# An adaLN block with a state-space convolution on one core: the order of its first fifty microseconds

## The chip, the core and the metric

The kernel runs on one core of a Trainium2 chip. The metric is the device time of one execution in microseconds (us). The core has five engines that run their own instruction streams in order: TensorE (PE in the profile, with its weight loads as PEld), VectorE (DVE), ScalarE (ACT), GpSimd (POOL) and SyncE (SP), which here only issues DMA transfers. They wait for each other by semaphores. Before the change the kernel took 1075.2 us, the median of three runs (1074.22, 1075.2 and 1078.04).

## The reference

The input is u, 2048 positions by 640 channels, a condition vector c of 640 and a modulation weight of 640 by 3840. Cut to what matters:

```python
mod = (_silu(c) @ w_mod).reshape(c.shape[0], 6, 1, -1)
sa, ca, ga, sb, cb, gb = (mod[:, i] for i in range(6))
h = _layernorm(u) * (1 + ca) + sa
# S4 convolution, for each channel d a kernel of 128 complex states, of length 2048
P = exp(dt * A * l);  K = einsum("dn,dnl,dn->dl", C, P, dt * B).real
y = irfft(rfft(pad(h)) * rfft(pad(K))) + h * Dskip
x = u + ga * y
h = _layernorm(x) * (1 + cb) + sb
out = x + gb * ((silu(h @ w1) * (h @ w3)) @ w2)     # F = 1728
```

## The kernel before

The kernel has a prelude, a loop of steps that makes the convolution, and an MLP that takes the second half of the time.

**The steps.** The 640 channels are 40 steps of 16 channels. The exponential of a step is split into a slow and a fast factor, so that the kernel K of 2048 positions comes from two tables of 32 and 64 places. For each step s:

- `exps(s)` makes the exponents of two steps at once. PE multiplies logarithms (`lah`, `lal`, `lmh`, `lml`) with constant ramps (`r2`, `r1`, `sel`) into PSUM tiles `pa` (L396) and `pq` (L408); ACT takes the exponential into tile `A`. `pa` and `pq` use the same two PSUM buffers (tag "A"), so `pq` waits until ACT has read `pa`, and the next `pa` until ACT has read `pq`.
- `phases(s)` makes integer phases on POOL (L419, L420); `absph(s)` and `trig(s)` make cosine and sine on ACT (`cs`, `ph`). Sine and exponential are in different ACT tables, and changing between them is an ACT_TABLE_LOAD.
- `tables(s)` on DVE (L438 to L441) multiplies exponentials with cosine and sine into `E` and `A`; `kgen(s)` (L450) and `k_stage1(s)` (L467) on PE turn these into the kernel's spectrum.

**The modulation.** `w_mod` is multiplied with silu(c) in 8 groups of up to 256 columns before the loop and 5 groups of 384 columns in it. `mod_sums` (L267) is one group: five matmuls, one for each 128 rows of c, each with 32 output partitions, at four column places of the PE array in turn; the fifth goes on the first place again. DVE copies the sums (`part`, L269), two small matmuls turn them into columns (L278) and DVE copies these (`cols`, L279). `mod_early(0..4)` make the shift sa and scale ca; `mod_shift` (L284 to L303) then computes sa / (1 + ca), a row `rrow` by PE (`pr`) and a first transform `shift` by PE (`ps`). `mod_early(5..7)` and `mod_gate` make the gate ga.

**The first transform of the input.** `ln1_load(j)` loads one of 16 tiles of 128 positions (seven buffers). `ln1_norm(p)` makes mean and variance of tiles 2p and 2p+1 on DVE (L345, L346, L349), their scale on POOL (L347, L348), and applies both on ACT in place (`x<-x,rs`). `u_stage1(j)` multiplies the tile with a 32-point transform in eight small matmuls (L374), 32 rows by 64 columns of the array each: `pu[0]` (PSUM tag "Z", one buffer) takes rows 0 to 63, `pu[1]` (tag "A") rows 64 to 127. For even j four further matmuls (L366) bring the constant `rrow` into `pu[0]` first, on the same places that the tile's first four need. ACT copies `pu[0]` of an even tile (L377, in the profile L116 `u<-pu`), DVE adds `shift` to the others (L379, L380). The result goes to a scratch in DRAM (L381, 640 KB a tile), from which the loop reads it channel by channel.

**The order.** A tile framework places instructions on each engine. It may move work of one engine past other work by its own priorities. ACT's activations and copies are kept in the order of the program, and so are the phases of steps 1 to 3 on POOL. A block `with tc.issue_after(ins)` holds instructions behind a given one. SP issues transfers in order, each waiting for the buffer that it writes. The gate's weights (`wg`) are loaded into the room of groups 0 to 2 and so wait until these have been multiplied.

Before the change, the prelude reads:

```python
for i, t in enumerate(("pb", "pk", "pb", "pk", "pb")):
    mod_early(i, wm[i], t)
...
mod_shift()
exps(0); ln1_norm(0); exps(2); ln1_norm(1)
phases(1); phases(2); absph(0); trig(0)
u_stage1(0); u_stage1(1); ln1_norm(2)
absph(1); trig(1)
```

What follows is `mod_early(5..7)`, `mod_gate`, `u_stage1(2)`, `u_stage1(3)`, the second half of the parameters (`rest = polar(d1, G)`, partly on POOL, L211 to L259) and the loop. Lines quoted here and in the prediction are those of the kernel before.

Of the kernel before, what the change touches and what calls it, by code (L numbers as in the profile page):

```python
# [9 lines left out]
F32 = mybir.dt.float32  # L10
# [7 lines left out]
P = 128  # L18
# [74 lines left out]
def tile_kernel(ctx: ExitStack, tc: tile.TileContext, a):  # L93
# [96 lines left out]


# [6 lines left out]
    for t, n in ((misc, "misc"), (iota, "iota"), (ident, "ident")):  # L198
        nc.sync.dma_start(t, a[n])

# [61 lines left out]
    def mod_sums(w, pm):  # L262

        n = w.shape[2]
        for k in range(KD):
            g = slice(k % 4 * NA, k % 4 * NA + NA)
            PE.matmul(pm[g, :n], scb[:, k], w[:, k, :], start=(k < 4), stop=(k > 0), tile_position=(0, g.start))  # L267
        part = pm_.tile([P, WC], F32, name="part", bufs=2)
        V.tensor_copy(part[:, :n], pm[:, :n])  # L269
        return part  # L270
# [60 lines left out]
    hpz = pre.enter_context(tc.tile_pool(name="hpz", bufs=2, side="right"))  # L331
    xt = [None] * NT

    def ln1_load(j):
        xt[j] = hpz.tile([P, D], F32, name="x", bufs=7)
        nc.sync.dma_start(xt[j], a["x"][j * P:(j + 1) * P, :])

# [19 lines left out]
    def u_stage1(j):  # L357


        x = xt[j]  # L360
        u = hpz.tile([P, 4, D // 2], F32, name="u", bufs=2)
        pu = [psS.tile([P, 2, 512], F32, name="pu", tag=t, bufs=n) for t, n in (("Z", 1), ("A", 2))]
        one = j % 2 == 0
        for q in range(2 if one else 0):
            for hh in range(2):
                PE.matmul(pu[0][hh * 64:hh * 64 + 64, q, :320], c1[q * NA:q * NA + 1],  # L366
                          rrow[q * NA:q * NA + 1, hh * 320:hh * 320 + 320],
                          start=True, stop=False, tile_position=(q * NA, hh * 64))
        for h in range(2):
            for q in range(2):  # L370
                r0 = (2 * h + q) * NA
                r = slice(r0, r0 + NA)
                for hh in range(2):
                    PE.matmul(pu[h][hh * 64:hh * 64 + 64, q, :320], s1r[r], x[r, hh * 320:hh * 320 + 320],  # L374
                              start=not (one and h == 0), stop=True, tile_position=(r0, hh * 64))
        if one:
            acopy(u[:, :2, :], pu[0][:, :, :320])  # L377
        else:
            V.tensor_tensor(u[:, :2, :], pu[0][:, :, :320], bc(shift, 1, 2), op=OP.add)  # L379
        V.tensor_tensor(u[:, 2:, :], pu[1][:, :, :320], bc(shift, 1, 2), op=OP.add)  # L380
        nc.sync.dma_start(usw[:, 4 * j:4 * j + 4, :], u)  # L381
# [4 lines left out]
    def exps(s, between=()):  # L386
# [18 lines left out]
        for i, (w, rt) in enumerate(((lah, r1), (lal, r1), (lmh, None), (lml, None))):  # L405
            for h, rr, r in rows:
                rv = bc(sel[r, js], 2, NA) if rt is None else rt[r, js, :]
                PE.matmul(pq[h][:, rr, :256], w[r, ch, :], rv,  # L408
                          start=(i == 0), stop=(i == 3), tile_position=(r.start, 0))
        for h in range(2):  # L410
            act(A[h].rearrange("p (r j) s b -> p r j s b", r=2)[:, :, :, 1, :],
                pq[h][:, :, :256].rearrange("p r (j b) -> p r j b", j=8), AF.Exp)
            AA[s + h] = A[h]

# [209 lines left out]
    for j in range(4):  # L624
        ln1_load(j)
# [5 lines left out]
    for i, t in enumerate(("pb", "pk", "pb", "pk", "pb")):  # L631
        mod_early(i, wm[i], t)
    nc.sync.dma_start(s1, a["s1"])
    nc.sync.dma_start(i2, a["i2"])
    nc.sync.dma_start(dz[0:P:NA], a["D"].rearrange("o (g q) -> (o q) g", q=4))
    wg = [w_load(w_room(1, i, n, 1280), 1280 + 256 * i) for i, n in enumerate((256, 256, 128))]
# [3 lines left out]
    mod_shift()  # L640
    exps(0)
    ln1_norm(0)
    exps(2)
    ln1_norm(1)
    phases(1)
    phases(2)
    absph(0)
    trig(0)
    u_stage1(0)
    u_stage1(1)  # L650
    ln1_norm(2)
    absph(1)
    trig(1)
# [360 lines left out]
```

## Time and profile before

| what | value |
| --- | --- |
| median of three runs | 1075.2 us |
| the profiled execution | 1072.31 us |
| its span, first to last instruction | 1070.2 us |
| mean granted TensorE clock | 0.932 |
| PE busy | 975.6 us, 91% |
| DVE busy | 626.6 us, 59% |
| ACT busy | 514.8 us, 48% |
| POOL busy | 266.5 us, 25% |

The profile is of one execution; its time is 2.9 us below the median of the runs. Busy PE counts pipelined matmuls to their ends, so it is not PE at its peak. In a timeline, each row is one or several like instructions: start, time from first start to last end, engine, line, operation, tiles, count, and in brackets the idle time before it with what ended it. ACT's instructions go through two helpers and stand at L113 (activations) and L116 (copies). A fp32 matmul leaves two records. The granted clock of a stretch is a share of PE's full speed. The chain of work that ended last goes from engine to engine through the prelude and the loop, and from about 470 us on stays on PE, in the MLP.

### The profile page before, as it was taken

The page shows a single profiled execution, that of the slowest core. Times are in us where ns is not written, and L with a number is a line of the kernel's source. Part 1 is how long each engine was busy: PE and PEld are TensorE (multiplying, and loading weights), DVE is VectorE, ACT ScalarE, POOL GpSimd, SP SyncE. Part 2 cuts the span into 40 slices and gives each one's busy share as a digit, 9 for nine tenths or more (in the row PEclk, how much of TensorE's full clock was granted, in tenths as well). Part 3 has the DMA queues.
Part 4 walks back from the last instruction along what each step waited for, and adds up shares of the span by engine and source line. Part 5 has one row for each costly group of instructions (what it writes and reads, how often), then busy time and mean ns, then how long its engine had stood idle before and what let it go on. Part 6 is the DMA issues. An engine that isn't in the chain of part 4 may idle for free.

```text
span 1070.2 us, 20346 instructions
## 1 busy us (share of the span) xinstructions
PE 975.6 (91%) x8324; PEld 721.4 (67%) x8324; DVE 626.6 (59%) x1024; ACT 514.8 (48%) x697; POOL 266.5 (25%) x213
## 2 busy tenths in 40 slices
PE   5898887888888899759999999999999999999997
PEld 2444455656665667437778877778777788788886
DVE  4698786787778877655543464443555543533332
ACT  3659585778777873233233432334432334333231
POOL 1633443453345412131211111211111211111110
PEclk9856699988899899869999999999999999999999
DMA  9373593454354549867543364443353233433311
GB/s 276 135 258 125 187 223 110 119 140 130 98 131 130 126 128 227 260 186 221 137 122 87 97 206 120 119 113 97 97 175 99 85 92 95 141 94 99 97 39 49
DMA packets 107040, 146.29 MB, mean 137 GB/s; under 512 B 20836, under 2 KB 62948, under 8 KB 106948
## 3 DMA queue, kind: packets, MB, share of 16 engines
q1 hardware_dynamic: 104500, 140.09, 45.3%
q0 software_dynamic: 1024, 2.49, 0.9%
q10 hardware_dynamic: 1424, 2.43, 0.8%
q8 instruction: 65, 1.06, 0.4%
q14 instruction: 27, 0.22, 0.1%
HBM read 118.76 MB, written 26.21 MB: 135 GB/s over the span
## 4 chain that ended last, share of the span: by engine, by line
PE 74%; DVE 12%; ACT 8%; DMA 3%; issue 2%; POOL 0%; SPq 0%; ACTq 0%; DVEq 0%; POOLq 0%
PE acc L875 17%; PE pg L861 6%; PE pg L862 6%; PE pg L863 6%; PE pu L863 6%; PE pu L862 6%; PE pu L861 6%; PE p L493 5%; PE pz L528 3%; PE pk L450 3%; DVE E L438 2%; PE pt L467 2%; PE pq L408 2%; PE pa L396 2%; DVE A L440 2%
## 5 line engine op out<-in xcount | busy, mean ns | idle before, releaser
L894 POOL TENSOR_TENSOR w<-w,gbr 128x512 f32<-128x512 f32 x55 | 85.1, 1547 | 402.6 <-DMA w<-in_w_dram 383.4
L419 POOL TENSOR_TENSOR ph<-thi,iota 128x1024 int32<-128x1024 int32 x40 | 83.3, 2082 | 194.5 <-DVE A L441 124.2
L861 PE MATMUL pg<-xh,gh 128*128 128x512 f32 x280 | 113.4, 405 | 0.1
L862 PE MATMUL pg<-xl,gh 128*128 128x512 f32 x280 | 111.1, 397 | 0.9 <-DVE xl L834 0.9
L863 PE MATMUL pg<-xh,gl 128*128 128x512 f32 x280 | 110.7, 395 | 0.0
L846 ACT CAST gh<-wg 128x640 fp32r<-128x640 f32 x55 | 40.0, 728 | 145.3 <-PE pg L862 137.8
L847 DVE TENSOR_TENSOR gl<-wg,gh 128x640 fp32r<-128x640 f32 x55 | 51.2, 930 | 92.4 <-ACT gh L846 90.2
L861 PE MATMUL pu<-xh,uh 128*128 128x512 f32 x260 | 102.8, 396 | 0.0
L863 PE MATMUL pu<-xh,ul 128*128 128x512 f32 x260 | 102.8, 396 | 0.0
L862 PE MATMUL pu<-xl,uh 128*128 128x512 f32 x260 | 102.8, 395 | 0.0
L847 DVE TENSOR_TENSOR wl<-w,wh 128x640 fp32r<-128x640 f32 x55 | 47.8, 868 | 89.5 <-ACT wh L846 89.5
L910 DVE TENSOR_TENSOR hf<-pu,sg 128x512 f32<-128x512 f32 x52 | 36.0, 692 | 108.7 <-PE pu L863 107.6
L846 ACT CAST uh<-wu 128x640 fp32r<-128x640 f32 x51 | 37.1, 727 | 111.3 <-issue 70.5
L875 PE MATMUL acc<-wh,hh 128*128 128x512 f32 x224 | 87.7, 391 | 0.0
L875 PE MATMUL acc<-wl,hh 128*128 128x512 f32 x224 | 87.2, 389 | 0.0
L493 PE MATMUL p<-uk,s 128*64 128x256 f32 x640 | 83.8, 407 | 1.3 <-DMA s<-in_s_dram 1.3
L438 DVE TENSOR_TENSOR E<-A,cs 128x1024 f32<-128x1024 f32 x40 | 62.3, 1558 | 37.7 <-ACT cs L113 32.1
L846 ACT CAST wh<-w 128x640 fp32r<-128x640 f32 x55 | 39.9, 726 | 92.2 <-PE acc L875 92.2
L875 PE MATMUL acc<-wh,hl 128*128 128x512 f32 x208 | 81.1, 390 | 0.0
L450 PE MATMUL pk<-E 128*32 128x64 f32 x1280 | 54.3, 247 | 17.8 <-DVE K L458 17.8
L861 PEld LDWEIGHTS pg<-xh,gh 128*128 128x128 f32 x280 | 52.6, 188 | 19.0 <-issue 5.6
L450 PEld LDWEIGHTS pk<-E 128*32 128x32 f32 x1280 | 38.7, 124 | 39.2 <-issue 30.9
(203 smaller groups left out, 2119.2 us busy)
## 6 DMA issues: line engine op xcount, KB each, us to landing
wg<-in_wg_dram SPq DMA_DIRECT2D x55, 320.0 KB
wu<-in_wu_dram SPq DMA_DIRECT2D x51, 320.0 KB
w<-in_w_dram SPq DMA_DIRECT2D x51, 320.0 KB
us<-u SPq DMA_DIRECT2D x16, 640.0 KB
s<-in_s_dram SPq DMA_DIRECT2D x40, 256.0 KB
i<-in_i_dram SPq DMA_DIRECT2D x40, 256.0 KB
uk<-us SPq DMA_DIRECT2D x32, 256.0 KB
zs<-zt SPq DMA_DIRECT2D x32, 256.0 KB
```

The lines of the kernel that those rows point to most:

```text
L419: keep(G.tensor_tensor(p, bc(thi[:, sl], 2, NPH), bc(iota, 1, SD), op=OP.mult))
L438: V.tensor_tensor(E[:, :, 1:3, :], A[:, :, 1:3, :], mid(c), op=OP.mult)
L450: PE.matmul(pk[dq * 32:dq * 32 + 32, g, :], x[:, g * 4 + dq, 1, :], x[:, g * 4 + dq, 0:3:2, :], start=(st == 0), stop=(st == 1), tile_posi ...
L493: PE.matmul(p2[par * 64:par * 64 + 64, pi, c, :], s2[:, pi * 2 + par, c * 64:c * 64 + 64], uk[:, 0:kn + 1:kn, f, :], start=True, stop=True ...
L846: S.copy(hi, src)
L847: V.tensor_tensor(lo, src, hi.bitcast(F32), op=OP.subtract)
L861: PE.matmul(ps, wh, xh, start=(i == 0), stop=False)
L862: PE.matmul(ps, wh, xl, start=False, stop=False)
L863: PE.matmul(ps, wl, xh, start=False, stop=(i == n - 1))
L875: PE.matmul(acc[k], lhs, rhs, start=(f == 0 and i == 0), stop=(f == NFT - 1 and i == len(terms) - 1))
L894: G.tensor_tensor(w2r[:, :512], w2r[:, :512], gbr, op=OP.mult)
L910: V.tensor_tensor(hf, pu, sg, op=OP.mult)
```

## The change

Six things are changed in the text of the kernel:

1. The first four input tiles are loaded ahead of the modulation weights instead of after them.
2. `exps(0)` comes after the first modulation group, `exps(2)` after `ln1_norm(0)`. Groups 1 and 2 are held behind the last matmul of `exps(0)`, groups 3 and 4 behind that of `exps(2)`.
3. `absph` and `trig` of steps 0 and 1 come before `mod_shift`, which stood ahead of the exponents. (`absph(0)` and `trig(0)` work on one step's phases; their ACT instructions are those of before.)
4. `ln1_norm(1)` and `phases(1)`, `phases(2)` move between them.
5. In `mod_sums`, the fifth matmul is two matmuls of half the columns, on the first and the second place.
6. In `u_stage1`, matmuls of `pu[0]` and `pu[1]` are issued in turn; for even tiles the constant rows alternate with those of `pu[1]`, and the tile's matmuls of `pu[0]` follow.

`exps` returns its last matmul for the holds. No operand or size of another operation is changed.

```diff
+    for j in range(4):
+        ln1_load(j)
     wm = [w_load(w, 256 * i) for i, w in enumerate(
...
     def mod_sums(w, pm):
         n = w.shape[2]
-        for k in range(KD):
-            g = slice(k % 4 * NA, k % 4 * NA + NA)
-            PE.matmul(pm[g, :n], scb[:, k], w[:, k, :], start=(k < 4), stop=(k > 0), tile_position=(0, g.start))
+        for k in range(KD - 1):
+            g = slice(k * NA, k * NA + NA)
+            PE.matmul(pm[g, :n], scb[:, k], w[:, k, :], start=True, stop=(k > 1), tile_position=(0, g.start))
+        for i in range(2):
+            g, c = slice(i * NA, i * NA + NA), slice(i * n // 2, (i + 1) * n // 2)
+            PE.matmul(pm[g, c], scb[:, KD - 1], w[:, KD - 1, c], start=False, stop=True, tile_position=(0, g.start))
...
         one = j % 2 == 0
-        for q in range(2 if one else 0):
-            for hh in range(2):
+        group = [(q, hh) for q in range(2) for hh in range(2)]
+        def part(h, q, hh):
+            r0 = (2 * h + q) * NA
+            r = slice(r0, r0 + NA)
+            PE.matmul(pu[h][hh * 64:hh * 64 + 64, q, :320], s1r[r], x[r, hh * 320:hh * 320 + 320],
+                      start=not (one and h == 0), stop=True, tile_position=(r0, hh * 64))
+        for q, hh in group:
+            if one:
                 PE.matmul(pu[0][hh * 64:hh * 64 + 64, q, :320], c1[q * NA:q * NA + 1],
                           rrow[q * NA:q * NA + 1, hh * 320:hh * 320 + 320],
                           start=True, stop=False, tile_position=(q * NA, hh * 64))
-        for h in range(2):
-            for q in range(2):
-                r0 = (2 * h + q) * NA
-                r = slice(r0, r0 + NA)
-                for hh in range(2):
-                    PE.matmul(pu[h][hh * 64:hh * 64 + 64, q, :320], s1r[r], x[r, hh * 320:hh * 320 + 320],
-                              start=not (one and h == 0), stop=True, tile_position=(r0, hh * 64))
+            else:
+                part(0, q, hh)
+            part(1, q, hh)
+        if one:
+            for q, hh in group:
+                part(0, q, hh)
...
-    for j in range(4):
-        ln1_load(j)
...
-    for i, t in enumerate(("pb", "pk", "pb", "pk", "pb")):
-        mod_early(i, wm[i], t)
     nc.sync.dma_start(s1, a["s1"])
     nc.sync.dma_start(i2, a["i2"])
     nc.sync.dma_start(dz[0:P:NA], a["D"].rearrange("o (g q) -> (o q) g", q=4))
+    mod_early(0, wm[0], "pb")
+    last = exps(0)
+    ln1_norm(0)
+    with tc.issue_after(last.ins):
+        mod_early(1, wm[1], "pk")
+        mod_early(2, wm[2], "pb")
+    last = exps(2)
+    with tc.issue_after(last.ins):
+        mod_early(3, wm[3], "pk")
+        mod_early(4, wm[4], "pb")
     wg = [w_load(w_room(1, i, n, 1280), 1280 + 256 * i) for i, n in enumerate((256, 256, 128))]
     for j in range(4, 7):
         ln1_load(j)
     nc.sync.dma_start(prm[:, :, d1], prma[:, :, d1])
-    mod_shift()
-    exps(0)
-    ln1_norm(0)
-    exps(2)
-    ln1_norm(1)
     phases(1)
-    phases(2)
     absph(0)
     trig(0)
+    ln1_norm(1)
+    absph(1)
+    trig(1)
+    mod_shift()
+    phases(2)
     u_stage1(0)
     u_stage1(1)
     ln1_norm(2)
-    absph(1)
-    trig(1)
     for i, t in enumerate(("pb", "pk", "pb")):
         mod_early(5 + i, wg[i], t)
     mod_gate()
```

## The prediction

> **What bounds the kernel now.** I read the page first, then the granted clock, the ScalarE (ACT) timeline of the first 135 us, the waits and the chain there, and stretches of 10 us. The change touches only what is issued before and early in the loop of steps, so the question is how soon that loop gets going. The page, busy tenths in 40 slices of 26.8 us:
>
> ```profile
> span 1070.2 us, 20346 instructions
> ...
> DVE  4698786787778877655543464443555543533332
> ACT  3659585778777873233233432334432334333231
> PEclk9856699988899899869999999999999999999999
> ```
>
> From the fifteenth slice on, PE alone is busy and the change alters nothing. Before that, several engines take turns, and the first slices are ragged. Next the ACT timeline (start, us, instruction, idle before it and what ended that):
>
> ```profile
> 14.67 1.28 ACT L113 ACT_TABLE_LOAD   x1
> 25.13 1.02 ACT L113 ACTIVATE A<-pa 128x1024 f32<-128x1024 f32 x1 [9.18 <-PE pa L396]
> 28.80 1.02 ACT L113 ACTIVATE A<-pa 128x1024 f32<-128x1024 f32 x1 [2.64 <-PE pa L396]
> ...
> 37.42 1.94 ACT L113 ACTIVATE A<-pa 128x1024 f32<-128x1024 f32 x2 [2.92 <-PE pa L396]
> ...
> 47.08 0.67 ACT L116 COPY u<-pu 128x640 f32<-128x640 f32 x1
> ...
> 59.57 0.69 ACT L116 COPY u<-pu 128x640 f32<-128x640 f32 x1 [7.11 <-PE pu L374]
> ...
> 76.98 1.74 ACT L113 ACTIVATE x<-x,rs 128x640 f32<-128x640 f32 x2 [3.85 <-DVE rs L349]
> ```
>
> ACT stands 9.18, 2.64 and 2.92 us for the `pa` matmuls of the exponents, since PE does five modulation groups between them; 7.11 us for the transform of tile 2; and 3.85 us for the norm of tiles 8 and 9. From 76.98 to 103 it has no wait over 0.4 us. Then PE, in stretches (PE, weight loads, DVE, ACT, POOL busy; clock; DMA share; GB/s):
>
> ```profile
> 10.00:20.00 10.00, 9.08 (x41) 3.80 (x37) 8.39 (x23) 5.12 (x9) 2.98 (x2) 1.00 1.09 339
> 20.00:30.00 10.00, 10.00 (x44) 5.28 (x46) 2.40 (x10) 2.05 (x2) 0.00 (x0) 1.00 0.98 294
> ...
> 40.00:50.00 10.00, 8.89 (x64) 3.83 (x60) 5.12 (x12) 9.84 (x12) 6.50 (x8) 0.67 0.25 91
> 50.00:60.00 10.00, 9.63 (x62) 3.63 (x60) 9.74 (x15) 2.86 (x4) 8.02 (x8) 0.50 0.31 108
> 60.00:70.00 10.00, 9.89 (x119) 4.47 (x120) 8.95 (x14) 8.23 (x12) 1.48 (x3) 0.50 0.90 311
> ```
>
> And two groups of PE's timeline (one modulation group of five matmuls, ten records; eight matmuls of the transform, sixteen records):
>
> ```profile
> 16.56 1.92 PE L267 MATMUL pm<-uk,scb 128*32 128x256 f32 x10 [0.25 <-DVE cols L279]
> 60.04 1.64 PE L374 MATMUL pu<-x,misc 32*64 32x320 f32 x16
> ```
>
> DVE is nearly idle from 20 to 30 (2.40 busy) and half idle from 40 to 50 (5.12), then full from 50 to 100: its work is there too late rather than too large. A modulation group takes 1.92 at 16.56, and two take 3.62 at 43.12 under a granted 0.50 to 0.67, so the 1.00 of the first stretches is no faster; I use one set of PE durations.
>
> **The change, step by step** (times of the profiled execution; after = my walk through the built order).
>
> *x ahead of its weights.* 1.31 MB of x now lies before the modulation weights. They landed at 9.82 (PE's first wait); at 339 and 227 GB/s (stretches 10 to 20 and 0 to 10) they come 3.9 to 5.8 later, 13.7 to 15.6. The group behind takes 1.5, done by 17.1 at worst; the exponents' first matmul needs DVE's `lml`, 16.8. Cost 0 to 0.3; I take 0. On SP the four issues took 3.02 at 12.03; the weights' issues move behind them by that, inside the transfers' delay. The gate weights on SP overwrite weights of groups 0 to 2 and now wait for them until about 25 instead of 18 to 22.6; behind them stand x tiles 4 to 6 and the second parameters. 1.94 MB at 339 GB/s and 2 us of issue make tile 6 land at 32.5; DVE wants it from 35. The 1.57 MB of parameters come near 37; POOL used them at 48.53. Hidden, with 2.5 us to spare; without that cover DVE would stand at tile 4's statistics, and the shift behind it would be later by as much.
>
> *Exponents first.* `pa` begins at 16.8, its second half behind the pair of column matmuls (L278) of group 0, which waits for DVE's `part` at 18.2 and takes 0.93: 19.2. In the trace 0.84 lies from the last `pa` to ACT (27.96 to 28.80): 20.05 against 25.13. Two exps 1.02 each; `pq` follows the freed buffer, 1.27 to ACT (85.79 to 87.06), the other half 0.9 later: the first pair of steps ends at 23.9, against 31.98. Norm of tiles 0 and 1 (1.65) to 25.5. PE meanwhile has groups 1 and 2 from 23.0 (below 1.28 each) and two pairs of 0.93: last `pa` at 27.85, exps from 28.7, end 32.6 against 41.2. So 8.6 early. On POOL the phases of step 1 (1.90 + 1.04 at 35.34) now stand ahead of the scale of tiles 2 and 3; that is ready near 26 and wanted at 37, so hidden by 11 us.
>
> *Trigonometry.* Steps 0 and 1 then cost ACT 1.05, 1.28 (table), 1.1, 1.0 and, around the norm of tiles 2 and 3 (1.65), 1.05, 1.1, 1.0. End 41.8 against 52.46: 10.7 early. DVE's tables of step 0 start near 38.4 instead of 49.79; there POOL's 128x512 work made them 2.31 instead of 1.12 us, which now falls after them.
>
> *What waits in exchange.* Groups 3 and 4 come after both exponents: 31.7 to 36.4 with their pairs. On DVE the reciprocal of the shift stands behind `E` of step 0, which waits for the sine at 36.05; L288's product comes at 40.3 (32.76 before), then 2.39 for `pr`, 1.41 for `ps`, 0.5 for the copy: shift at 44.6 against 37.25, 7.35 late. Behind it are `u` of tiles 0 and 1, and behind those their stores and the loads of tiles 7 and 8. Constant rows and tile 0 on PE, two rounds of 1.07: ACT copies tile 0 at 46.4, against 47.08. Only 0.7 is left of the lead, and ACT stands 4.6 us for it.
>
> *It comes back.* Tile 2 needs its norm (48.6), groups 6 and 7 between, the freed Z buffer and two rounds: 54.4 against 59.57, lead 5.2. DVE no longer has step 0's tables in between (5.7 us there). Tile 4: 59.6 against 65.08, 5.5. Tile 6: 65.4 against 72.46, 7. In the built order the norm of tiles 8 and 9 now stands ahead of three `u` additions that it stood behind: 66.1 against 76.98, 10.9. The DMA lets less through: from 60 to 80 it moved 311 and 281 GB/s, and a tile's store and load are 0.96 MB, 3.2 us; from the first store (47) the eighth is not before 69.4, against 76.9: 7.5.
>
> *Fifth matmul halved.* A group is four rounds of 0.43 (weight loads at 16.56, 16.99, 17.41); two of them have one place busy. If the halves overlap it saves 0.43, if not 0; columns next to each other overlap in the same row, so I take 0.43, inside the 1.28. Five later groups of 384 columns save 0 to 0.64 each, and the chain passes through two: 0 to 1.3, I take 0.5.
>
> *Eight places.* Sixteen records (eight matmuls) at 60.04 took 1.64, two rounds and the latency, so they overlapped already. For even tiles the constant rows need the same places as half the tile in either order. Ends: 0, and 1.07 for each of the 16; I take 0.
>
> *Sum.* The lead at 77 is between 5.2 and 10.9. I take 7.5 by the DMA and 0.5: 8.0. Behind that ACT, then DVE and PE go round in turn with nothing tied to absolute time, so it stays. The profiled execution took 1072.3 with 1070.2 of span; less 8.0 that is 1064.3. The median of the three runs is 2.9 above it: **1067.2**.
>
> **A rule against the rows.** PE from 50 to 70 is busy 9.63 and 9.89 of 10 us, at granted 0.50. The Trainium skill, "TensorE: Matmul & The Clock Gate", section "Why this matters for your kernels", says that over 4 us of continuous work bring the full clock; the trace disagrees there, so the sum does without it. By that rule the result would be the rival "clock" below.
>
> **Rivals.**
> - *Shift decides* (slower). If the transform path, not tables and ACT, sets the end of the prelude, the shift's 7.35 us of delay is paid: 1072.3 + 7.35 + 2.9 = 1082.5. It decides once tile 2 is copied later than 59.57; my walk has 5.2 us to that. For it: `pu` of tile 0 was ready at 43.2, and comes at 46.3. Against: ACT could use it only at 47.08, and PE then waited for DVE's tables.
> - *Lead eaten* (same). The lead stays at the 0.7 of tile 0 up to about 2 us, because stores, loads and half-clock PE fill what DVE and ACT leave: -2, 1073.2. For it: PE 8.9 to 9.9 busy from 40 to 80, DMA 0.90 from 60 to 70. Against: the leads of 5.2 to 10.9 worked out above.
> - *Clock* (faster). The denser PE runs at full clock from 32 to 46: groups, `pr`, `ps` and tile 0, some 9.7 us, halve; 4.8 more: 1062.4. Against: rows above.
>
> **How the numbers follow.** Forecast as summed (5.5 to 11 kept) 0.54; clock 0.08; lead eaten 0.24; shift decides 0.14. About 0.5%, 5.4 us, is what a measurement of this kernel can tell from no change. Faster 0.62, same 0.24, slower 0.14. The range goes from the clock's case with the larger lead, 1060, over the eaten lead to 1076, and leaves out most of the slower case.
>
> **What would show it.** Right: ACT's first exp near 20, step 0's first `E` near 38 to 40, tile 0's copy near 46, tile 2's before 56, the ACT norm of tiles 8 and 9 between 65 and 70, and the loop's later steps 7 to 9 us earlier. Wrong: group 0's weights after 17, tile 2's copy after 59, DVE standing at `E` of step 0 with the reciprocal behind it, or an early lead that is gone by 130 us with DMA over 0.9 or a lower granted clock.

## The result: slower by half a per cent

The changed kernel takes 1081.33 us, the median of 11 runs (1077.71 to 1086.84), beside 1076.22 us for the kernel before in the same comparison (11 runs, 1073.10 to 1079.95). The ratio is 1.005, with a 95% interval of 1.0029 to 1.0072: 5.1 us slower, where 8 us less were forecast. The profiled execution took 1084.09 us with a span of 1082.3.

From here on, lines are those of the changed kernel or of the experiment named. In the changed kernel the norm of two input tiles is L350 to L354 (L345 to L349 before), the phases on POOL L433 and L434 (L419, L420), the shift L296 to L315, the tables on VectorE (DVE) L452 to L455 (L438 to L441).

The page of the changed kernel, busy tenths in 40 slices of 27.1 us:

```profile
span 1082.3 us, 20399 instructions
...
DVE  6599775887789778556444365344455543533332
ACT  4468683788778874233224333234432243433331
PEclk9566587888899999969999999999999999999999
```

VectorE works more in the first slice and less in the second (6 and 5 where it had 4 and 6), so something came forward and something behind it did not. The ACT timeline of the changed kernel (start, us, instruction, idle before it and what ended that) tells how far it got:

```profile
20.48 1.94 ACT L113 ACTIVATE A<-pa 128x1024 f32<-128x1024 f32 x2 [4.16 <-PE pa L409]
...
31.60 1.94 ACT L113 ACTIVATE A<-pa 128x1024 f32<-128x1024 f32 x2 [5.65 <-PE pa L409]
...
43.46 1.04 ACT L113 ACTIVATE ph<-ph 128x1024 f32<-128x1024 int32 x1
54.18 0.69 ACT L116 COPY u<-pu 128x640 f32<-128x640 f32 x1 [9.68 <-PE pu L374]
...
64.33 0.69 ACT L116 COPY u<-pu 128x640 f32<-128x640 f32 x1 [7.83 <-PE pu L374]
...
78.23 1.73 ACT L113 ACTIVATE x<-x,rs 128x640 f32<-128x640 f32 x2
```

The first exponent is 4.65 us earlier, the end of the trigonometry of step 1 (44.5) 8 us earlier than before. Then ACT stands 9.68 us for tile 0 and 7.83 us for tile 2: tile 0 is copied 7.1 us later than before, tile 2 4.8 us later, and the norm of tiles 8 and 9, expected at 66, stands at 78.23. What held tile 0 is in the DVE timeline of the changed kernel:

```profile
21.91 1.86 DVE L354 SCALAR_TENSOR_TENSOR rs<-mv,rs 128x2 f32<-128x2 f32 x1 [0.74 <-POOL rs L353]
...
25.97 1.85 DVE L354 SCALAR_TENSOR_TENSOR rs<-mv,rs 128x2 f32<-128x2 f32 x1 [1.09 <-POOL rs L353]
27.75 0.41 DVE L281 COPY part<-pm 128x256 f32<-128x256 f32 x1
...
42.92 1.17 DVE L452 TENSOR_TENSOR E<-A,cs 128x1024 f32<-128x1024 f32 x1
44.01 0.18 DVE L299 RECIPROCAL cols<-cols 128x5 f32<-128x5 f32 x1
44.96 1.85 DVE L354 SCALAR_TENSOR_TENSOR rs<-mv,rs 128x2 f32<-128x2 f32 x1 [0.77 <-POOL rs L353]
46.74 0.68 DVE L453 TENSOR_TENSOR E<-A,cs 128x512 f32<-128x512 f32 x1
47.34 1.00 DVE L300 TENSOR_TENSOR cols<-cols 128x5 f32<-128x5 f32 x1
48.26 1.21 DVE L454 TENSOR_TENSOR A<-A,ph 128x1024 f32<-128x1024 f32 x1
49.40 1.55 DVE L307 TENSOR_TENSOR part<-misc,cols 128x320 f32<-128x320 f32 x1
...
52.85 0.49 DVE L315 COPY shift<-ps 128x320 f32<-128x320 f32 x1 [0.84 <-PE ps L313]
...
64.45 0.16 DVE L354 SCALAR_TENSOR_TENSOR rs<-mv,rs 128x2 f32<-128x2 f32 x1 [0.63 <-POOL rs L353]
```

and in the POOL timeline of the same execution:

```profile
21.84 1.91 POOL L433 TENSOR_TENSOR ph<-thi,iota 128x1024 int32<-128x1024 int32 x1
...
25.91 1.90 POOL L433 TENSOR_TENSOR ph<-thi,iota 128x1024 int32<-128x1024 int32 x1
...
44.90 1.90 POOL L433 TENSOR_TENSOR ph<-thi,iota 128x1024 int32<-128x1024 int32 x1
46.88 1.44 POOL L434 TENSOR_TENSOR ph<-ph,phi 128x512 int32<-128x512 int32 x1
48.28 2.32 POOL L220 TENSOR_TENSOR uk<-uk 128x512 f32<-128x512 f32 x1
```

L354 multiplies two pairs of numbers in each partition. It takes 0.16 us at 64.45 and 1.85 us in these three places. Each time, POOL has just finished the scale that L354 waits for (L353) and begins the phases of a step in the same tenth of a microsecond; L354 ends when they do (21.91 + 1.86 = 23.77, 21.84 + 1.91 = 23.75). L300 (0.15 us in the experiment with the product on POOL) and L307 (0.48 there) are stretched in the same way beside L434 and L220. The first stall only pushes back the statistics of tiles 2 and 3, which are ready at 24.88, when POOL is free for them. The second holds the copy of modulation group 1 (27.75); TensorE waits 2.15 us for it, and group 2, the second pair of exponents and groups 3 and 4 come behind. The third stands in the middle of the shift.

The chain of work that ended last, between 44 and 53 us, is this queue:

```profile
44.23 0.71 POOL rs L353
...
44.96 1.85 DVE rs L354
46.81 0.60 DVE E L453
47.41 0.93 DVE cols L300
48.34 1.13 DVE A L454
49.47 1.48 DVE part L307
...
51.00 1.83 PE ps L313 x10
...
52.85 0.49 DVE shift L315
```

Last, the stretches from 14 to 42 us and from there to the last of the 24 additions of the shift, the end of the first transform (PE, weight loads, DVE, ACT, POOL busy and their instructions; clock; DMA share; GB/s). The kernel before:

```profile
14.00:42.00 28.00, 25.83 (x157) 15.11 (x160) 13.17 (x46) 10.61 (x17) 10.59 (x10) 0.96 0.71 230
42.00:126.70 84.70, 71.79 (x818) 35.93 (x808) 74.56 (x132) 62.74 (x76) 36.34 (x33) 0.62 0.49 176
```

The changed kernel:

```profile
14.00:42.00 28.00, 21.56 (x143) 13.54 (x143) 15.07 (x41) 16.71 (x23) 10.64 (x10) 0.77 0.74 225
42.00:131.00 89.00, 74.08 (x851) 38.85 (x849) 79.72 (x139) 57.65 (x70) 38.16 (x34) 0.62 0.46 167
```

VectorE has about the same instructions (178 and 180). Its idle time fell by 2.8 us (25.0 to 22.2), its busy time rose by 7.1 (87.7 to 94.8), and the transform ends 4.3 us later: near the 5.1 us of the medians. Two things limit such comparisons. The two profiled executions lie 11.8 us apart (1072.31 and 1084.09), so some microseconds between two profiles need not be a difference of the kernels. And the clock of the first stretches says little: the clock records begin at 36.4 us in the profile before and at 25.6 us in the changed one, and what lies ahead of them counts as 1.00. So the question for the experiments is which of three it is: the late shift, VectorE's stalls beside POOL, or the parts that touch only TensorE's matmuls.

### The profile page after: what moved, and what is told of

Same layout as the page of the kernel before. It is cut to its first block, busy times and chain, and to the rows that moved or that the text cites. A ratio compares the mean times of both kernels' runs of the same rounds, so it can differ in the third digit from the quotient of the medians.

```text
span 1082.3 us, 20399 instructions
## 1 busy us (share of the span) xinstructions
PE 979.3 (90%) x8350; PEld 729.7 (67%) x8350; DVE 632.7 (58%) x1024; ACT 515.1 (48%) x697; POOL 267.7 (25%) x213
## 3 DMA queue, kind: packets, MB, share of 16 engines
q1 hardware_dynamic: 104500, 140.09, 44.5%
q8 instruction: 66, 1.08, 0.4%
## 4 chain that ended last, share of the span: by engine, by line
PE 75%; DVE 12%; ACT 6%; DMA 3%; issue 2%; POOL 0%; SPq 0%; DVEq 0%; ACTq 0%; POOLq 0%
PE acc L892 17%; PE pg L878 6%; PE pg L879 6%; PE pg L880 6%; PE pu L878 6%; PE pu L880 6%; PE pu L879 6%; PE p L507 5%; PE pz L542 3%; PE pt L481 3%; PE pk L464 3%; DVE E L452 2%; PE pq L421 2%; PE pa L409 2%; DVE A L454 2%
## 5 line engine op out<-in xcount | busy, mean ns | idle before, releaser
L433 POOL TENSOR_TENSOR ph<-thi,iota 128x1024 int32<-128x1024 int32 x40 | 83.3, 2082 | 202.8 <-DVE A L455 127.3
L864 DVE TENSOR_TENSOR gl<-wg,gh 128x640 fp32r<-128x640 f32 x55 | 53.4, 971 | 93.1 <-ACT gh L863 91.1
L892 PE MATMUL acc<-wh,hh 128*128 128x512 f32 x224 | 87.7, 391 | 0.0
L452 DVE TENSOR_TENSOR E<-A,cs 128x1024 f32<-128x1024 f32 x40 | 62.2, 1556 | 38.1 <-ACT cs L113 32.1
L481 PE MATMUL pt<-s,K 128*64 128x128 f32 x640 | 59.3, 315 | 10.4 <-ACT uk L116 10.1
L507 PEld LDWEIGHTS p<-uk,s 128*64 128x64 f32 x640 | 46.5, 148 | 30.0 <-issue 11.4
```

The lines of the kernel that those rows point to most:

```text
L433: keep(G.tensor_tensor(p, bc(thi[:, sl], 2, NPH), bc(iota, 1, SD), op=OP.mult))
L452: V.tensor_tensor(E[:, :, 1:3, :], A[:, :, 1:3, :], mid(c), op=OP.mult)
L481: PE.matmul(pt[c * 64:c * 64 + 64, g, :], kk[:, g, :], s1[:, c, :], start=True, stop=True, tile_position=(0, c * 64))
L507: PE.matmul(p2[par * 64:par * 64 + 64, pi, c, :], s2[:, pi * 2 + par, c * 64:c * 64 + 64], uk[:, 0:kn + 1:kn, f, :], start=True, stop=True ...
L864: V.tensor_tensor(lo, src, hi.bitcast(F32), op=OP.subtract)
L892: PE.matmul(acc[k], lhs, rhs, start=(f == 0 and i == 0), stop=(f == NFT - 1 and i == len(terms) - 1))
```

## The experiments

All ratios are to the kernel before on the same chip, with 95% intervals; 0.1% is 1.08 us.

### The parts of the change by themselves

**e1: parts 5 and 6 alone.** The kernel before, with

```diff
-        for k in range(KD):
+        for k in range(KD - 1):
...
-        for h in range(2):
-            for q in range(2):
...
+        for q, hh in group:
...
```

> The kernel before, with only parts 5 and 6 of the change (the halved fifth matmul and the order of the transform's matmuls); the order of the prelude is that of before. If the late shift is the cause (theory): within 0.3% of before, 1073 to 1079; a group of five matmuls takes about 1.5 us instead of 1.92, tile 0 and tile 2 are copied within 1 us of 47.1 and 59.6. If the halves or the eight places do the harm (rival): 1079 to 1084, with the loop's steps 3 to 5 us late although the prelude's first 50 us are as before.

1079.20 us, 1.0029 (1.0012 to 1.0046). Tile 0 is copied at 45.4 and tile 2 at 58.1, 1.7 and 1.4 us earlier than before (the theory allowed 1 us), and still it is some 3 us slower, on the border of both expectations. The loss does not sit in the prelude: in its profile step 3's tables begin 0.9 us earlier than before, and the tables are 3 us late only from step 16 on.

**e2: parts 1 to 4 alone**, the changed kernel with both functions as before:

```diff
-        for k in range(KD - 1):
+        for k in range(KD):
...
-        for q, hh in group:
...
+        for h in range(2):
+            for q in range(2):
...
```

> The changed kernel without parts 5 and 6: exponents, trigonometry, x loads and holds as changed, matmuls in the order of before. If the late shift is the cause: 1079 to 1084 like the changed kernel, shift ready at 53 to 54, tile 0 copied at 54 to 55, tile 2 at 64 to 65. If halves or places do the harm: 1073 to 1078, like before.

1077.18 us, 1.0009 (0.9985 to 1.0033). The shift comes at 52.2 and tile 2 at 62.2, nearly as late as in the changed kernel, but the time is that of before. The theory's 1079 to 1084 is missed, and the other side's 1073 to 1078 is met: a late shift alone did not make this order slower than before.

**e7: part 5 alone.** The kernel before, with

```diff
-        for k in range(KD):
-            g = slice(k % 4 * NA, k % 4 * NA + NA)
...
+        for i in range(2):
+            g, c = slice(i * NA, i * NA + NA), slice(i * n // 2, (i + 1) * n // 2)
```

> The kernel before with part 5 alone, the halved fifth matmul. If part 5 carries the 2.9 us of e1: 1078 to 1081. If the order of the transform's matmuls (part 6) does: 1075 to 1077. If each carries some: 1077 to 1078.

1074.58 us, 0.997 (0.9946 to 0.9994): a small gain, below all three expectations.

**e9: part 6 alone.** The kernel before, with

```diff
-        for h in range(2):
-            for q in range(2):
...
+        for q, hh in group:
...
```

> The kernel before with part 6 alone, the order of the transform's matmuls. e7 (part 5 alone) came out at 0.997 of before and e1 (parts 5 and 6) at 1.0029, so if the two add up, part 6 alone costs about 0.6%: 1081 to 1084. If part 6 only takes back what part 5 gives (together no gain, alone no loss): 1075 to 1078.

1077.58 us, 1.001 (0.9983 to 1.0037). So parts 5 and 6 do not seem to add up: −0.3% and +0.1% by themselves, +0.3% together, a gap of 0.5% where the three intervals together allow about 0.4%. The runs show no cause for it.

**e15: part 1 alone.** The kernel before, with

```diff
+    for j in range(4):
+        ln1_load(j)
     wm = [w_load(w, 256 * i) for i, w in enumerate(
...
-    for j in range(4):
-        ln1_load(j)
```

> The kernel before with part 1 alone, input tiles 0 to 3 loaded ahead of the modulation weights. As priced in the prediction (nothing): within 2 us of before, 1074 to 1079, with the groups 4 to 6 us later but the tables of step 0 near 50 as before. If the delayed weights hold groups, shift and everything behind them: tile 0 copied at 50 to 53, time 1080 to 1083.

1074.48 us, 0.9982 (0.9965 to 0.9999). The shift comes at 41.3 instead of 37.3 and tile 0 at 50.8 instead of 47.1, and nothing is lost by it: the time is as the first expectation said although tile 0 is as late as the second did. It is a first sign that a shift 4 us late is not paid.

### The shift

**e3: the shift ahead of the second exponents.** The changed kernel, with

```diff
     with tc.issue_after(last.ins):
         mod_early(1, wm[1], "pk")
         mod_early(2, wm[2], "pb")
-    last = exps(2)
-    with tc.issue_after(last.ins):
         mod_early(3, wm[3], "pk")
         mod_early(4, wm[4], "pb")
+    mod_shift()
+    exps(2)
...
-    mod_shift()
```

> The changed kernel, but groups 1 to 4 are all held behind the first exponents only, and the shift (reciprocal to transform) follows them, ahead of the second exponents, the later loads and all phases and trigonometry. If the late shift is the cause: shift ready at 36 to 41, tile 0 copied at 38 to 43, tile 2 at 50 to 58, exponents of the second pair end 4 to 6 us later than in the changed kernel (34.8), and the time falls by 5 us or more below the changed kernel, to 1070 to 1076. If early exponents have another price (x ahead of the weights, colder PE): the shift comes early as said, but the time stays at 1079 to 1083.

1085.0 us, 1.0072 (1.0045 to 1.0099): with e13 the slowest of all, and above both expectations. The shift is 8.4 us earlier than in the changed kernel (44.95), but the second pair of exponents ends at 46.2 instead of 35.5, and since ACT's copies stay behind the trigonometry in program order, tile 0 still comes at 55.2 and tile 2 at 67.9. An earlier shift, not as early as expected, is worth nothing here because ACT cannot take tile 0.

**e8: the shift late.** e4 (below), with the weights of groups 3 and 4 loaded behind input tiles 4 to 6, and the groups with them:

```diff
-    wm = [w_load(w, 256 * i) for i, w in enumerate(
-        [w_room(1, 0, 256, 1280), w_room(1, 1, 256, 1280), w_room(1, 2, 256, 1280), w_table(), w_table()])]
+    wm = [w_room(1, 0, 256, 1280), w_room(1, 1, 256, 1280), w_room(1, 2, 256, 1280), w_table(), w_table()]
+    for i in range(3):
+        w_load(wm[i], 256 * i)
...
     for j in range(4, 7):
         ln1_load(j)
+    for i in (3, 4):
+        w_load(wm[i], 256 * i)
```

> e4_scale_on_pool, with the weights of modulation groups 3 and 4 loaded behind input tiles 4 to 6, so that the shift alone comes later: exponents of the second pair still end near 33, the first tables still begin near 40 to 41, but the shift is ready at 50 to 55 instead of 45.8. If the shift's lateness is paid at the end (theory): tile 2 is copied at 58 to 63 instead of 53.2, and the time is 4 to 8 us above e4, 1076 to 1080. If exponents and tables set the time: tile 2 late as said, the time within 2 us of e4, 1070 to 1074.

1069.23 us, 0.9936 (0.9906 to 0.9965). The shift is 6.8 us later than in e4 (52.6 against 45.8), tile 2 8.2 us later, and the time is not above e4's 0.9959 (on another chip, each against the kernel before there). The theory fell here. What the run did besides: the framework put both steps' first tables into the hole in front of the shift (37.6 and 44.5, against 40.4 and 54.1 in e4), so less of VectorE's work stood behind it.

**e11: the same edit on e10** (below).

> e10 with the weights of groups 3 and 4 loaded behind input tiles 4 to 6, as e8 is to e4: the shift 5 to 8 us later, the tables of step 1 ahead of it. If a late shift costs nothing by itself, as e8 against e4 said: within 3 us of e10. If e8 only had a lucky granted clock (0.941 on the mean against 0.932): 4 to 7 us above e10.

1070.98 us, 0.9936 (0.9916 to 0.9955), e10 0.9954. Again not slower, and on the same chip as e10, so a lucky clock in e8 is not needed to explain it. The ACT timeline of e11:

```profile
52.98 0.69 ACT L116 COPY u<-pu 128x640 f32<-128x640 f32 x1 [10.94 <-PE pu L383]
...
60.29 0.69 ACT L116 COPY u<-pu 128x640 f32<-128x640 f32 x1 [4.99 <-PE pu L383]
```

ACT stands 10.94 us for tile 0, longer than in the changed kernel, at no cost that the ratio shows. Tile 2 follows 8.6 us after the shift (11.0 in the changed kernel).

**e13: both steps' tables ahead of the shift.** The changed kernel, with

```diff
     trig(1)
+    tables(0)
+    tables(1)
     mod_shift()
...
-        if tk < NS:
+        if 2 <= tk < NS:
             tables(tk)
```

> The changed kernel with the tables of steps 0 and 1 ahead of the shift in the program; nothing else moved. If the shift's lateness were what is paid: shift ready at 57 to 60 instead of 53, time 4 to 6 us above the changed kernel, 1085 to 1088. If VectorE's work and idle time up to 90 us set the time: step 1's tables at 46 to 50 instead of 64.5, step 3's within 2 us of the changed kernel's 91.05, time 1078 to 1083.

1084.22 us, 1.007 (1.0051 to 1.0089), inside neither: the shift comes at 62.8 and tile 2 at 74.2, and by the medians the kernel is 2 to 3 us slower than the changed one, though the intervals overlap.

**e14: the same edit on e6** (below).

> e6 (parts 1 to 4, small product on POOL) with the tables of steps 0 and 1 ahead of the shift. If VectorE's work and idle time set the time and the shift does not: step 3's tables within 2 us of e6's 83.9, time 1064 to 1069, whatever the shift does. If a later shift costs: 1071 to 1075.

1080.78 us, 1.0045 (1.0025 to 1.0064), e6 0.9906 and 0.9936: 12 to 15 us lost, more than either expectation. The shift is 12.7 us later (59.9), and the ACT timeline of e14 shows where it goes:

```profile
60.91 0.69 ACT L116 COPY u<-pu 128x640 f32<-128x640 f32 x1 [18.27 <-PE pu L379]
...
70.96 0.69 ACT L116 COPY u<-pu 128x640 f32<-128x640 f32 x1 [7.73 <-PE pu L379]
```

So the opposite theory, that the place of the shift is free altogether, fell too. Between 60 us and the tables of step 3, VectorE stands 7.5 us in e14 and not at all in e6.

**e17: the late shift on e6**, the edit of e8 there.

> e6 (parts 1 to 4, small product on POOL) with the weights of groups 3 and 4 loaded behind input tiles 4 to 6, as in e8 and e11. If a shift that is 5 us later costs nothing as long as tile 2 is copied before about 62, and the gap on VectorE is filled with the tables of step 0: within 3 us of e6. If it costs: 4 to 7 us above e6.

1073.28 us, 0.997 (0.9946 to 0.9993), beside 0.9936 for e6 on the same chip: 3.7 us more, between both expectations and at the edge of what the intervals can tell. Here tile 2 comes at 65.25, 5 us later than in e11 with nearly the same shift (52.0 and 51.7).

Read together: of the twelve profiles with the changed order of exponents (not e3), eight copy tile 2 between 53.2 and 62.2, with ratios of 0.9906 to 1.0009 in no order; four copy it later than 64 (e17 65.3, the changed kernel 64.3, e14 71.0, e13 74.2) at 0.997, 1.005, 1.0045 and 1.007. A late shift was hidden where tile 2 still came by 61 us (e8, e11) and paid where it came at 71 (e14). Where between them it begins to cost, the runs do not fix: e17, at 65.3, is faster than e2 at 62.2. The changed kernel, at 64.3, lies in this gap; that part of its loss is its late tile 2 is likely, not shown. What made the tile 10 us later than forecast is the next question.

### VectorE beside POOL

**e4: L354 on POOL.** The changed kernel, with

```diff
-        V.scalar_tensor_tensor(rs[:, 2, :], mv[:, :, 0], -1.0, rs[:, 1, :], op0=OP.mult, op1=OP.mult)
+        G.tensor_tensor(rs[:, 2, :], mv[:, :, 0], rs[:, 1, :], op=OP.mult)
+        G.tensor_tensor(rs[:, 2, :], rs[:, 2, :], neg1[:, 0:1].broadcast_to([P, 2]), op=OP.mult)
```

> The changed kernel, but the small product of mean and 1/std of the input norm (128x2) runs on POOL as two products instead of on DVE, so that DVE does not stand at it while POOL makes its integer phases. If DVE standing beside POOL is what made the shift later than predicted: the products take well under 0.5 us each off DVE's queue, the second pair of exponents ends 2 to 3 us earlier (near 32), the shift is ready near 48 to 50 instead of 53, tile 2 is copied near 60, and the time is 2 to 4 us below the changed kernel. If the delay comes only from where the shift stands in DVE's order: shift at 52 to 53 and the time within 1.5 us of the changed kernel.

1072.17 us, 0.9959 (0.9941 to 0.9978): 9 us below the changed kernel and 4 below the kernel before. The shift comes 7.5 us earlier (45.8), tile 2 11.2 us earlier (53.2), more than expected of 3 x 1.85 us. Some of that belongs to this execution: it took 1065.94 us, 6.2 below the median, and TensorE was granted full speed from 43.6 us on, so that `pr` and `ps` took 1.89 and 0.99 us against 2.39 and 1.83 in the changed kernel. The DVE timeline of e4:

```profile
40.41 1.17 DVE L455 TENSOR_TENSOR E<-A,cs 128x1024 f32<-128x1024 f32 x1
41.50 0.18 DVE L301 RECIPROCAL cols<-cols 128x5 f32<-128x5 f32 x1
41.59 0.65 DVE L456 TENSOR_TENSOR E<-A,cs 128x512 f32<-128x512 f32 x1
42.16 0.15 DVE L302 TENSOR_TENSOR cols<-cols 128x5 f32<-128x5 f32 x1
42.24 1.22 DVE L457 TENSOR_TENSOR A<-A,ph 128x1024 f32<-128x1024 f32 x1
43.37 0.48 DVE L309 TENSOR_TENSOR part<-misc,cols 128x320 f32<-128x320 f32 x1
```

From the first table to the shift's products nothing is stretched now, because POOL begins its next phases (at 43.87) only when these are nearly through; the order of VectorE's instructions is that of the changed kernel. The waiting has moved to POOL: from 40.64 its four small products take 1.00, 1.09, 0.63 and 0.33 us beside VectorE's tables, where at 21.10 they took 0.20, 0.71, 0.20 and 0.20. The stretches of e4:

```profile
14.00:42.00 28.00, 23.61 (x155) 13.90 (x157) 14.18 (x47) 19.27 (x25) 12.62 (x16) 0.78 0.76 229
42.00:120.00 78.00, 65.45 (x834) 35.77 (x828) 72.34 (x126) 55.09 (x67) 43.78 (x44) 0.65 0.54 191
```

VectorE is busy 86.5 us instead of 94.8, with seven instructions fewer, and the transform ends 11 us earlier, 9 us by the medians of the whole time.

**e12: only the third stall taken away.** As e4, from the third pair of tiles on:

```diff
+        if p < 2:
             V.scalar_tensor_tensor(rs[:, 2, :], mv[:, :, 0], -1.0, rs[:, 1, :], op0=OP.mult, op1=OP.mult)
+        else:
+            G.tensor_tensor(rs[:, 2, :], mv[:, :, 0], rs[:, 1, :], op=OP.mult)
...
```

> The changed kernel with the norm's small product on POOL only from the third pair of tiles on; the two stalls of DVE at 21.9 and 26.0 stay, the one at 45.0, in the middle of the shift and the tables of step 0, goes. If the third stall carries most of e4's gain of 9 us: 1073 to 1076. If the first two do, by the second exponents: 1079 to 1082. If each takes its 1.8 us share and what lies beside POOL: 1076 to 1079.

1075.29 us, 0.9982 (0.9962 to 1.0002). It takes back 6 us of the 9, by the medians, as the first expectation said; that the other two stalls carry the rest is within the noise. The second pair of exponents still ends at 36.0, but the product of the shift and the shift itself come so:

```profile
43.74 0.16 DVE L302 TENSOR_TENSOR cols<-cols 128x5 f32<-128x5 f32 x1
...
47.94 0.49 DVE L317 COPY shift<-ps 128x320 f32<-128x320 f32 x1 [0.41 <-PE ps L315]
```

4.9 us earlier than in the changed kernel; tile 2 is copied at 56.8, 7.5 us earlier.

**e5: the edit of e4 on the kernel before**, at L349.

> The kernel before, with the small product of the norm (128x2) on POOL as in e4_scale_on_pool. If DVE standing beside POOL costs only in the changed order, where three norms meet POOL's phases instead of one (the trace of before shows 1.85 us once, at 45.61): 1074 to 1077, within 2 us of before. If the product on POOL is worth as much in any order (later norms too): 1066 to 1069, 7 to 10 us below before.

1078.51 us, 1.0009 (0.9991 to 1.0028): nothing. In the old order the trace has only one such stall (1.85 us at 45.61), and it isn't worth anything there:

```profile
45.61 1.85 DVE L349 SCALAR_TENSOR_TENSOR rs<-mv,rs 128x2 f32<-128x2 f32 x1 [0.79 <-POOL rs L348]
...
64.08 0.16 DVE L349 SCALAR_TENSOR_TENSOR rs<-mv,rs 128x2 f32<-128x2 f32 x1 [0.86 <-POOL rs L348]
```

The profile of e15, also in the old order, has two (at 28.3 and 44.4), and e15 lost nothing. So the price belongs to the changed order.

**e6 and e18: e4 without parts 5 and 6**, the edit of e2 on e4; one kernel, run twice.

> e4_scale_on_pool without parts 5 and 6 of the change. If those two parts cost 3 to 4 us in any order, as the pairs e1 against before (+2.9) and changed kernel against e2 (+4.1) say: 1067 to 1070. If their cost came from the lateness of those two orders: 1071 to 1074, like e4.

> e6 once more, beside e17 on the same chip. If its 0.9906 was no accident of its few runs: 0.988 to 0.994, 1064 to 1070. If parts 5 and 6 make no difference in this order and e6 was lucky: 0.995 to 0.997, like e4 and e10.

1066.43 us, 0.9906 (0.9876 to 0.9936, 6 runs), and 1069.86 us, 0.9936 (0.9911 to 0.9960, 12 runs). This is the fastest version found: 7 to 10 us below the kernel before by the ratios of two comparisons. Beside e2 it repeats the test of e4, since only the small product differs: 8 to 11 us. Over all profiles with the changed order, the second pair of exponents ends at 34.5 to 36.0 us in the four with the first two stalls (changed kernel, e2, e12, e13) and at 32.3 to 34.8 in the eight without. Where nothing else moved the shift, it comes at 52.2 and 53.3 us with the third stall (e2, changed kernel) and at 45.8 to 49.7 without (e4, e6, e18, e10, e12).

**e10: e4 without part 6**, with

```diff
-        for q, hh in group:
...
+        for h in range(2):
+            for q in range(2):
...
```

> Parts 1 to 5 of the change with the norm's small product on POOL, that is e4 without part 6. If part 6 costs 5 to 6 us and part 5 gains 2 to 3 also here: 1063 to 1067, the fastest so far. If part 5 was the harm in this order (e6 leaves both out): 1070 to 1073, like e4.

1073.17 us, 0.9954 (0.9927 to 0.9980), like e4. So in this order no gain of the halved fifth matmul is seen (e10 against 0.9906 and 0.9936 for e6), while in the old order there was one (e7).

### The price of VectorE's time

**e16: VectorE longer.** The kernel before, with

```diff
-        V.tensor_tensor(E[:, :, 1:3, :], A[:, :, 1:3, :], mid(c), op=OP.mult)
+        for _ in range(3 if s < 2 else 1):
+            V.tensor_tensor(E[:, :, 1:3, :], A[:, :, 1:3, :], mid(c), op=OP.mult)
```

> The kernel before, with the first product of the tables made three times instead of once in steps 0 and 1: four further VectorE products of 1.2 us, 4.8 us (up to 9 where POOL works beside them). If VectorE bounds the stretch from 42 to 90 us: the time rises by 4 to 8 us, 1080 to 1085, and step 3's tables begin as much later. If VectorE has slack there and the shift's path or TensorE sets the end: 1075 to 1078.

1082.06 us, 1.006 (1.0038 to 1.0081). The four extra products took some 5 us; its DVE timeline for step 0, in which the first two of three are extra:

```profile
50.99 1.35 DVE L439 TENSOR_TENSOR E<-A,cs 128x1024 f32<-128x1024 f32 x1
...
53.37 1.22 DVE L439 TENSOR_TENSOR E<-A,cs 128x1024 f32<-128x1024 f32 x1
...
55.30 1.50 DVE L439 TENSOR_TENSOR E<-A,cs 128x1024 f32<-128x1024 f32 x1
```

Step 3's tables begin 6.2 us later (96.4 against 90.2), the last addition of the shift ends 6.2 us later (132.9), and the time rises by 6.5 us (4 to 9), as the first expectation said. VectorE's time between 51 and 73 us, where these products run, is paid about one to one.

Over all twenty profiles, before and changed kernel included, the time of a kernel (its ratio) goes with the end of its last addition of the shift: correlation 0.84, 0.98 us for each microsecond. With the time of the shift itself it does not (0.02). That last figure mixes two orders, though: among the twelve profiles with the changed order alone it is 0.78, beside 0.84 for the end of the transform. There a late shift and a late transform go together, and a correlation can't part them.

## Why the prediction was wrong, point by point

The prediction's own walk beside the changed kernel and e4, which differs from it only in where a 128x2 product runs (us):

| event | predicted | changed | e4 |
| --- | --- | --- | --- |
| first exponent | 20.05 | 20.48 | 20.69 |
| end of first pair | 23.9 | 24.3 | 24.5 |
| end of second pair | 32.6 | 35.5 | 32.9 |
| first table of step 0 | 38.4 | 42.9 | 40.4 |
| shift | 44.6 | 53.3 | 45.8 |
| tile 0 | 46.4 | 54.2 | 46.6 |
| tile 2 | 54.4 | 64.3 | 53.2 |
| tile 4 | 59.6 | 70.3 | 61.2 |
| norm of tiles 8 and 9 | 66.1 | 78.2 | 69.1 |

- **x ahead of its weights, cost 0: right.** The first `pa` begins at 17.05 (16.8 expected), group 0 is copied at 18.24; e15 shows no loss from the part alone.
- **Exponents first: right for the first pair, 2.9 us off for the second.** The step that failed: "On POOL the phases of step 1 ... hidden by 11 us". The scale of tiles 2 and 3 was indeed not late (25.9). But I asked only who waits for POOL's result, not what POOL's phases do to VectorE while they run. They held L354 twice, behind it the second time the copy of group 1, and TensorE stood 2.15 us for that at 28.21. With these stalls the second pair ends some 2 us later than without, on the mean of the profiles. I priced this term at nothing. Without it and the third stall the kernel is 9 us faster (e4 against the changed kernel) and 8 to 11 us faster (e6 and e18 against e2).
- **"POOL's 128x512 work made them 2.31 instead of 1.12 us, which now falls after them": right for that one table (1.17), wrong as a saving.** POOL's work did not go away, it met other instructions: L354 at 44.96, L300, L307. The 1.85 us were in the trace of before, at 45.61, and I did not read them. The table itself came 4.5 us later than walked: 2.9 from the second pair, and the rest because in the built order it stands behind the columns of group 4 (41.27) on VectorE, not only behind the sine.
- **Shift at 44.6, "7.35 late": 8.7 us short.** Groups 3 and 4 begin 3.0 later (the second pair), they and their columns take 6.5 us where I allowed 4.7 (part of tile 0's transform stands between them), the way on to L300 is 2.2 longer (mainly the third stall), and from L300 to the shift there are 6.0 where I had 4.3 (L300 and L307 beside POOL, and `ps` at 1.83 instead of 1.41). POOL is behind most of it but for the second term; e4, without the stalls, has the shift 7.5 us earlier, 1.3 of that by its faster `pr` and `ps`.
- **"It decides once tile 2 is copied later than 59.57; my walk has 5.2 us to that": the distance was eaten by the stalls.** Tile 2 came at 64.33, 9.9 us later than walked and past one of the prediction's own signs of being wrong (59); in e4, without the stalls, it comes at 53.2. The rival *shift decides* came nearly to the measured time (1082.5; 1081.3), but by luck: it adds a delay of 7.35 us paid in full, while the shift came 16.1 us later than before and the time rose by 5.1. The shift's delay paid in full is not how it works: e8 and e11 have a shift as late as 52 and lose nothing. If there is such a point, the runs place it only between 61 and 71 us.
- **"its work is there too late rather than too large": half right.** The lead at the norm of tiles 8 and 9 was kept in e4 (69.1, 7.9 early), yet the time fell by 4.1 us there. In e6 the lead at this norm is 4.4 us, in its repetition e18 2.1, and the time fell by 10 and 7. So that lead, which the sum took over to the end, does not measure the gain. The forecast 8 us less was reached only without the stalls and, as far as two comparisons tell, without parts 5 and 6; that the size agrees there is no proof of the sum. From 42 to 127 us VectorE was busy 74.6 of 84.7 us already before; e16 shows that more work for it there is paid about one to one.
- **Fifth matmul halved and eight places: near 0 by themselves (−0.3% and +0.1%), +0.3% together.** TensorE's part was read rightly: a group takes about 1.5 us at the lower clock (34.74 to 36.24) instead of 1.92. That it turns into 0.5 us at the end was no better than a guess: alone it gained (e7), in the changed order no gain is seen (e10). Why, stays open.
- **Clock.** The rival *clock* did not occur: from 30 to 42 us TensorE was busy 10.89 of 12 us at a granted 0.50. But "the 1.00 of the first stretches is no faster; I use one set of PE durations" was misread: that profile has no clock record before 36.4 us. At a recorded full speed a group takes 1.05 us (e18, at 50.86), not 1.92. One set of durations held here because TensorE ran at half speed from 29.0 to 52.9 us in the changed kernel.

In short: the forecast was 8 us less, the measurement 5.1 more. The stalls that the prediction left out are worth 9 of these 13 us by e4 against the changed kernel. The other 4 are about what parts 5 and 6 cost in this order: 4 us in the changed kernel against e2, 2 to 6 in e4 against e6 and e18. What stays open: how much of the stalls' price is the late shift and how much VectorE's longer busy time, since they cause both; and why parts 5 and 6 cost anything in company.

## What to carry to other kernels

When instructions of two engines are moved against each other, look at what they do to each other while both run, not only at who waits for whose result: here a product of 0.16 us became 1.85 us each time POOL's phases started beside it, in the middle of a chain. A late producer can be hidden up to some point (here with tile 2 as late as 61 us), and the distance to that point must include what the move itself slows down. And where several engines take turns, price a moved wait by the engine that is full afterwards, VectorE here, not by the one that was seen waiting.

## What the runs showed of the hardware

A VectorE instruction with two inputs in SBUF waits for a POOL product that began before it, however small it is. In the first 400 us of the profiles before and of the changed kernel, none that starts inside a POOL product of over 0.5 us (and at least 0.3 us before its end) ends before it: L354 (128x2) ends within 0.02 us of POOL's phases in all three places. Instructions with one such input are not touched: beside the phases at 16.23 to 18.17 us, the statistics of 128x320 took 0.49 and a subtraction with one input in PSUM (L263) 0.27 us, while the 128x128 product L267, begun at 17.12, took 1.20 us and ended 0.15 after POOL. The Trainium skill states this: "SBUF — State Buffer", section "Who interferes with whom", says that a VectorE instruction with two SBUF inputs contends with a GpSimd instruction that reads SBUF, that the lock is exclusive, and that the order of issue decides who blocks. The trace agrees, with 1.85 us against 0.16. It shows the other order of issue too: POOL's L352 (128x2), begun at 43.15 beside the table L452 of 42.92 to 44.09, takes 1.00 us instead of 0.20.

The same kernel does not start alike twice: e6 and e18 are one program, but TensorE's first recorded full speed lasts from 25.9 to 29.4 us in one profile and from 49.1 to 55.9 in the other; the first `pa` matmuls of the second pair took 0.50 and 0.80 us. The second pair of exponents ended at 32.3 and 34.8, the last addition of the shift at 123.2 and 125.3. A single profile of this kernel therefore tells times in the prelude to about 2.5 us.
